# The head of a six-layer cross network: the first column group of x0 through TensorE, the biases loaded later

## The chip, the cores and the metric

The kernel runs on one core of a Trainium2 chip. Its engines are TensorE (matrix multiplications; PE in the profile, PEld for its weight loads), VectorE (DVE), ScalarE (ACT), GpSimd (POOL) and SyncE (SP), which here only issues DMA transfers. ScalarE issues some transfers too. The metric is device microseconds of one execution; lower is better.

## The reference

The input x0 has 4096 rows of 416 values in bf16. Six layers follow, each with a 416x416 weight and a bias:

```python
x = x0
for l in range(ws.shape[0]):
    x = x0 * (x @ ws[l] + bs[l]) + x
return x
```

## The kernel before, in words

The kernel keeps x transposed: features lie on the 128 partitions, rows of x along the free axis. 416 features are three planes of 128 (`NK`) and a remainder of 32 (`R`). The 4096 rows are two halves (`s`) of four column groups (`g`) of 512 (`CW`). `XM[0]` holds the three planes of x0 for all rows, `XR[0]` the remainder, packed so that group g of a half lies on partitions 32g to 32g+31. `XRd` is the same with the upper and lower 64 partitions swapped.

How x0 gets there. Eight transposing loads (`load_x0t`, line 76) on SyncE's queue fill the planes, one for each group of each half; each brings 512 rows by 384 features from DRAM. The remainder of the first half comes by four small loads on ScalarE's queue (`load_xrem0`, line 81) with 64-byte pieces into `xrig`; TensorE transposes these four 128x128 tiles (`x0_rem`, line 157), and VectorE copies them out of PSUM three times (line 160): once to `XR[0]` and twice, by halves, to `XRd`. ScalarE's queue also carries the first layer's weights (line 72) and the biases `bsb` (line 102). The weight's last 32 rows (`WR`, line 88) come on SyncE's queue and are copied on chip to the other three partition groups, two by ScalarE (line 110) and one by GpSimd (line 112).

How TensorE starts. It first runs filler matmuls on a constant tile (line 141), eleven of them: two of 256 columns and nine of 512. Then `bias_setup` transposes the biases by seven small matmuls (lines 149 and 151), and VectorE copies them to `bM` and `bR` (lines 152 and 153). Then comes `first_layer(0)`: for each of three output blocks m three matmuls over the planes k for group 0 (line 214), the remainder's four transposes, the same nine matmuls for group 1, eight row matmuls (line 221, contraction over the 32 remainder features), and then groups 2 and 3, six matmuls to an output block. An output block of two groups is a PSUM tile of two banks; the pool has four such tiles, and a tile is taken again when its last reader is done. ScalarE takes the block out of PSUM with the bias added (line 165), VectorE multiplies by x0 and adds x (lines 166 and 169). The second half and the four middle layers follow in the same manner with 128x32 weight tiles (line 181), and the last layer runs the other way round and writes the output rows (lines 327 to 355).

What sets the order. Each engine runs its instructions in the order of its own queue, which a scheduler has laid out from the program; only instructions with `keep_in_program_order` stay where they are written. Waits are semaphore waits. Transfers share eight semaphore lanes in turn: a transfer waits, on its issuing queue, until the transfer that had its lane eight places earlier has landed. In this program the third transposing load waits in that way for the first one, the fourth for the bias load, and the last of the four remainder loads for the first layer's weights.

The lines that set up the head are these:

```python
load_x0t(0, 0)
load_wm(nc.scalar, 0)
nc.scalar.dma_start(bsb[:], bs[:, :])
load_x0t(0, 1)
load_xrem0()
load_wr0()
nc.scalar.activation(dz[:, 1:2], dz[:, 0:1], ACT.Identity, bias=dz[:, 0:1], scale=1.0)
```

The last of them is there to bring ScalarE's function table into the engine before it is needed.

Of the kernel before, what the change touches and what calls it, by code (L numbers as in the profile page):

```python
# [9 lines left out]
ACT = mybir.ActivationFunctionType  # L10
ALU = mybir.AluOpType
BF16 = mybir.dt.bfloat16
FP32 = mybir.dt.float32
# [3 lines left out]
def kernel(  # L17
# [7 lines left out]
    nc = tc.nc  # L25
    B, D = x0.shape
    L = ws.shape[0]
    P = 128
    NK = 3
    R = D - NK * P  # L30
    assert R == 32 and B == 4096 and D == 416 and L >= 2
    NS = 2
    NG = 4
    CW = 512
# [5 lines left out]
    big = ctx.enter_context(tc.tile_pool(name="big", bufs=1))  # L40
    tpool = ctx.enter_context(tc.tile_pool(name="tpool", bufs=6))
    opool = ctx.enter_context(tc.tile_pool(name="opool", bufs=10))
    psum = ctx.enter_context(tc.tile_pool(name="psum", bufs=4, space=bass.MemoryType.PSUM))

    x0_v = x0.rearrange("(bt p) d -> p bt d", p=P)
    out_v = out.rearrange("(bt p) d -> p bt d", p=P)

    ident = const.tile([P, P], BF16)
    dz = const.tile([P, 2], FP32)
    warm = const.tile([P, CW], BF16)  # L50
# [4 lines left out]
    bsb = const.tile([L, D], BF16)  # L55
# [4 lines left out]
    XLrows = big.tile([P, NBT, D], BF16)  # L60
    scrR = [big.tile([P, 4, P], BF16, name=f"scrR{s}") for s in range(NS)]
    xrem = big.tile([P, 16, R], BF16)
    xrig = big.tile([P, NS, 4, P], BF16)
    XRd = big.tile([P, NS * CW], BF16)
    XM = [big.tile([P, NK, B], BF16, name=f"XM{i}") for i in range(3)]
    XR = [big.tile([P, NS * CW], BF16, name=f"XR{i}") for i in range(3)]

    def col0(s, g):
        return SW * s + CW * g

    def load_wm(eng, l):
        eng.dma_start(WM[:, l], ws[l, 0:NK * P, :].rearrange("(k p) n -> p k n", p=P))

    def load_x0t(s, g):
        c0 = col0(s, g)
        nc.sync.dma_start_transpose(out=XM[0][:, :, c0:c0 + CW], in_=x0[c0:c0 + CW, 0:NK * P])  # L76

    def load_xrem0():
        with nc.allow_non_contiguous_dma(reason="64B row segments"):
            for i in range(4):  # L80
                nc.scalar.dma_start(xrig[:, 0, i, :].rearrange("p (g r) -> p g r", g=NG), x0_v[:, i:16:4, NK * P:D])

    def load_xrem1():
        with nc.allow_non_contiguous_dma(reason="64B row segments"):
            nc.sync.dma_start(xrem[:], x0_v[:, 16:32, NK * P:D])

    def load_wr0():
        nc.sync.dma_start(WR[0:R, 0, :], ws[0, NK * P:D, :])
# [8 lines left out]
    nc.gpsimd.memset(ones[:], 1.0)  # L97
    nc.gpsimd.memset(WD[:], 0.0)

    load_x0t(0, 0)  # L100
    load_wm(nc.scalar, 0)
    nc.scalar.dma_start(bsb[:], bs[:, :])
    load_x0t(0, 1)
    load_xrem0()
    load_wr0()
    nc.scalar.activation(dz[:, 1:2], dz[:, 0:1], ACT.Identity, bias=dz[:, 0:1], scale=1.0)  # L106
    for g in range(1, NG):
        dst, src = WR[32 * g:32 * g + 32, 0, :], WR[0:R, 0, :]
        if g < NG - 1:
# [2 lines left out]
            nc.gpsimd.tensor_copy(dst, src)  # L112
    for g in range(2, NG):
        load_x0t(0, g)
    load_x0t(1, 0)
    load_xrem1()
    for g in range(1, NG):
# [16 lines left out]
    nc.gpsimd.tensor_copy(xrig[:, 1].rearrange("p i (g r) -> p i g r", g=NG), xrem[:].rearrange("p (g i) r -> p i g r", g=NG))  # L134
    fill_wd(1, L)

    wps = psum.tile([P, CW], FP32, tag="ps", name="wps")

    def pe_filler(n, cols):
        for i in range(n):  # L140
            nc.tensor.matmul(wps[:, 0:cols], lhsT=warm[:, 0:P], rhs=warm[:, 0:cols], start=True, stop=True)  # L141

    pe_filler(2, 2 * P)
    pe_filler(8, CW)

    def bias_setup():
        pb = psum.tile([P, 4, 8], BF16, tag="ps", name="pb")
        for m in range(NK):
            nc.tensor.transpose(pb[:, m, 0:L], bsb[0:L, 128 * m:128 * m + 128], ident[0:L, 0:L])
        for g in range(NG):  # L150
            nc.tensor.transpose(pb[32 * g:32 * g + 32, 3, 0:L], bsb[0:L, NK * P:D], ident[0:L, 0:L], tile_position=(0, 32 * g))  # L151
        nc.vector.tensor_copy(bM[:], pb[:, 0:NK, 0:L])  # L152
        nc.vector.tensor_copy(bR[:], pb[:, 3, 0:L])

    def x0_rem(s, tpr):
        for i in range(4):
            nc.tensor.transpose(tpr[:, 128 * i:128 * i + 128], xrig[:, s, i, :], ident[:])  # L157
        for dst, src in ((slice(0, P), slice(0, P)), (slice(64, P), slice(0, 64)), (slice(0, 64), slice(64, P))):
            to = XR[0] if dst == src else XRd
            nc.vector.tensor_copy(to[dst, CW * s:CW * s + CW], tpr[src])  # L160

    def ew_main(l, s, m, h, pt, cur, nxt, pin=False):
        c0 = col0(s, 2 * h)
        t = tpool.tile([P, 2 * CW], BF16, name="t")
        nc.scalar.activation(t[:], pt[:].rearrange("p a b -> p (a b)"), ACT.Identity, bias=bM[:, m, l:l + 1], scale=1.0)  # L165
        prod = nc.vector.tensor_tensor(out=t[:], in0=t[:], in1=XM[0][:, m, c0:c0 + 2 * CW], op=ALU.mult)  # L166
        if pin:
            tc.keep_in_program_order(prod)
        nc.vector.tensor_tensor(out=nxt[:, m, c0:c0 + 2 * CW], in0=t[:], in1=cur[:, m, c0:c0 + 2 * CW], op=ALU.add)  # L169

    def ew_rem(l, s, pr, curR, nxtR):
        tr = tpool.tile([P, 2 * CW], BF16, name="t")
        nc.scalar.activation(tr[:, 0:CW], pr, ACT.Identity, bias=bR[:, l:l + 1], scale=1.0)  # L173
        nc.vector.tensor_tensor(out=tr[:, 0:CW], in0=tr[:, 0:CW], in1=XR[0][:, CW * s:CW * s + CW], op=ALU.mult)  # L174
        nc.vector.tensor_tensor(out=nxtR[:, CW * s:CW * s + CW], in0=tr[:, 0:CW], in1=curR[:, CW * s:CW * s + CW], op=ALU.add)  # L175
# [15 lines left out]
    def mm_rem(l, s, pr, cur, curR):  # L191
        for g in range(NG):
            nc.tensor.matmul(pr[32 * g:32 * g + 32, :], lhsT=WD[:, l, g, :], rhs=curR[:, CW * s:CW * s + CW],  # L193
                             start=True, stop=False, tile_position=(0, 32 * g))
        for k in range(NK):
            for g in range(NG):
                c0 = col0(s, g)
                nc.tensor.matmul(pr[32 * g:32 * g + 32, :], lhsT=WM[:, l, k, NK * P:D], rhs=cur[:, k, c0:c0 + CW],  # L198
                      start=False, stop=(k == NK - 1), tile_position=(0, 32 * g))
# [8 lines left out]
    def first_layer(s):  # L208
        cur, curR, nxt, nxtR = XM[0], XR[0], XM[1], XR[1]

        def full(pt, m, h, gl, after_row):
            c0 = col0(s, 2 * h + gl)
            for k in range(NK):
                nc.tensor.matmul(pt[:, gl, :], lhsT=WM[:, 0, k, 128 * m:128 * m + 128], rhs=cur[:, k, c0:c0 + CW],  # L214
                                 start=(k == 0 and not after_row), stop=(k == NK - 1 and after_row))

        def row(pt, m, h, opens):
            for gl in range(2):
                rg = 32 * ((2 * h + gl) ^ (2 if m == 1 else 0))
                src = XRd if m == 1 else curR  # L220
                nc.tensor.matmul(pt[:, gl, :], lhsT=WR[rg:rg + 32, 0, 128 * m:128 * m + 128],  # L221
                                 rhs=src[rg:rg + 32, CW * s:CW * s + CW],
                                 start=opens, stop=not opens, tile_position=(rg, 0))

        def ph(m):
            return psum.tile([P, 2, CW], FP32, tag="ps", name=f"ph{m}")

        pa = [ph(m) for m in range(NK)]
        if s == 0:
            for m in range(NK):  # L230
                full(pa[m], m, 0, 0, False)
            tp0 = psum.tile([P, CW], BF16, tag="ps", name="tpr")
            x0_rem(0, tp0[:])
            for m in range(NK):
                full(pa[m], m, 0, 1, False)
        else:
            for m in range(NK):
                for gl in range(2):
                    full(pa[m], m, 0, gl, False)
        pb = [ph(0)]  # L240
        row(pa[0], 0, 0, False)
        row(pb[0], 0, 1, True)
        row(pa[2], 2, 0, False)
        row(pa[1], 1, 0, False)
        for m in range(NK):
            ew_main(0, s, m, 0, pa[m], cur, nxt)
        for m in range(NK):
            if m:
                pb.append(ph(m))
            for gl in range(2):  # L250
                full(pb[m], m, 1, gl, m == 0)
        row(pb[1], 1, 1, False)
        row(pb[2], 2, 1, False)
        pr = psum.tile([P, 2, CW], FP32, tag="ps", name="pr")
        mm_rem(0, s, pr[:, 0, :], cur, curR)
        if s == 0:
            x0_rem(1, pr[:, 1, :].bitcast(BF16)[:, 0:CW])
        for m in range(NK):
            ew_main(0, s, m, 1, pb[m], cur, nxt, pin=(s == 0))
        ew_rem(0, s, pr[:, 0, :], curR, nxtR)  # L260

    bias_setup()
    pe_filler(1, CW)
    for s in range(NS):
        first_layer(s)

# [48 lines left out]
    l = LL  # L315
# [97 lines left out]
```

## Time and profile before

| | |
|---|---|
| Median of three runs | 130.97 us (130.72 to 131.04) |
| Profiled execution | 130.71 us |
| Its span, from first to last instruction | 128.9 us |
| Mean granted TensorE clock | 0.998 |
| TensorE busy | 123.1 us, 96% |
| VectorE busy | 107.1 us, 83% |
| ScalarE busy | 86.9 us, 67% |
| GpSimd busy | 5.9 us, 5% |
| 72 matmuls of line 214 (groups of layer 0) | 16.5 us busy |

Times in the profile count from the start of the span. A busy matmul row overlaps the next one, since matmuls are pipelined: the pitch between two, not the duration of one, is what a row of them costs. A line of the timeline has start, length, engine, source line, operation, tile written and tiles read, shape, count, and in brackets how long the engine stood idle before it and what ended that. The chain that ended last is followed back from the last instruction, at each step to what released it.

### The profile page before, as it was taken

To read this page: it belongs to the slowest core of one execution; us is meant where nothing else is said; L and a number is where in the kernel's file an instruction comes from. 1 tells how busy PE (TensorE), PEld (TensorE's weight loads), DVE (VectorE), ACT (ScalarE), POOL (GpSimd) and SP (SyncE) were. 2 spreads that over 40 slices of the span, in tenths; PEclk is the share of its full clock that TensorE was granted. 3 is DMA by queue.
4 is the path that set the end of the run, shared out by engine and by line. 5 is a ranking of instruction groups with operands and counts; after the bars stand their busy time and mean duration, and the time that the engine had idled before them with its cause. 6 is when DMAs were issued, how large, how long until landed. Compare 5 with 4: busy or idle time off the path is not lost.

```text
span 128.9 us, 3973 instructions
## 1 busy us (share of the span) xinstructions
PE 123.1 (96%) x1690; PEld 54.9 (43%) x1690; DVE 107.1 (83%) x197; ACT 86.9 (67%) x99; POOL 5.9 (5%) x18
## 2 busy tenths in 40 slices
PE   6999999999999999999999999999999999999960
PEld 2343443354444444444444444444444445445420
DVE  1032979999999898989898989898989899898991
ACT  0426783987848577848668848668847896569670
POOL 4022200600000000000000000000000000000000
PEclk9999999999999999999999999999999999999999
DMA  3999999999990000000000000000297999995754
GB/s 106 237 203 217 170 158 260 247 328 333 336 299 11 5 0 8 0 0 5 0 5 0 5 0 5 0 5 0 42 166 164 123 219 178 187 323 188 231 179 139
DMA packets 42102, 16.37 MB, mean 127 GB/s; under 512 B 30906, under 2 KB 42084, under 8 KB 42084
## 3 DMA queue, kind: packets, MB, share of 16 engines
q1 hardware_dynamic: 39416, 15.56, 54.6%
q10 hardware_dynamic: 2668, 0.56, 2.3%
q8 instruction: 13, 0.21, 0.7%
q14 instruction: 5, 0.04, 0.1%
HBM read 6.15 MB, written 3.41 MB: 74 GB/s over the span
## 4 chain that ended last, share of the span: by engine, by line
PE 80%; DMA 8%; DVE 5%; issue 2%; SPq 1%; ACT 1%; DVEq 0%
PE pt L181 49%; PE ph L214 9%; DMA XM<-in_x_dram 8%; PE py L327 8%; PE pt L187 5%; PE pr L198 5%; DVE t L355 3%; DVE o L344 2%; PE pr L193 2%; SPq L76 1%; PE py L333 1%; PE ph L221 1%; PE py L336 1%; ACT t L354 1%; PE pr L157 0%
## 5 line engine op out<-in xcount | busy, mean ns | idle before, releaser
L181 PE MATMUL pt<-XM,WM 128*32 128x512 bf16 x1152 | 65.2, 379 | 0.0
L165 ACT ACTIVATE t<-pt,bM 128x1024 bf16<-128x1024 f32 x48 | 49.6, 1115 | 18.3 <-PE pt L187 18.3
L166 DVE TENSOR_TENSOR t<-t,XM 128x1024 bf16<-128x1024 bf16 x60 | 41.4, 690 | 5.3 <-ACT t L165 5.3
L169 DVE TENSOR_TENSOR XM<-t,XM 128x1024 bf16<-128x1024 bf16 x60 | 41.8, 696 | 3.4
L181 PEld LDWEIGHTS <-WM 128*32 128x32 bf16 x1152 | 29.7, 97 | 33.8 <-issue 5.1
L354 ACT CAST t<-py 128x416 bf16<-128x416 f32 (+1 forms) x23 | 14.8, 642 | 4.8 <-PE py L327 2.1
L327 PE MATMUL py<-WM,XM 128*128 128x416 bf16 x96 | 17.7, 340 | 0.0
L214 PE MATMUL ph<-XM,WM 128*128 128x512 bf16 x72 | 16.5, 379 | 0.1
L165 ACT ACTIVATE t<-ph,bM 128x1024 bf16<-128x1024 f32 x12 | 12.5, 1114 | 4.4 <-PE ph L221 4.4
L327 PEld LDWEIGHTS <-XM 128*128 128x128 bf16 x96 | 9.0, 98 | 8.5 <-issue 1.4
L355 DVE TENSOR_TENSOR t<-t,X0rows 128x416 bf16<-128x416 bf16 (+1 forms) x23 | 10.4, 454 | 1.2 <-ACT t L354 1.2
L214 PEld LDWEIGHTS <-WM 128*128 128x128 bf16 x72 | 6.8, 98 | 8.6 <-issue 1.3
L344 DVE TENSOR_TENSOR o<-t,XLrows 128x416 bf16<-128x416 bf16 (+1 forms) x23 | 10.3, 451 | 0.0
L173 ACT ACTIVATE t<-pr,bR 128x512 bf16<-128x512 f32 x10 | 6.4, 684 | 2.7 <-PE pr L198 2.1
L198 PE MATMUL pr<-XM,WM 128*32 128x512 bf16 x120 | 8.2, 379 | 0.0
L187 PE MATMUL pt<-XR,WR 32*128 32x512 bf16 x96 | 7.3, 379 | 0.0
L141 PE MATMUL wps<-warm 128*128 128x512 bf16 (+1 forms) x11 | 4.4, 593 | 1.2 <-DVE warm L94 1.2
L175 DVE TENSOR_TENSOR XR<-t,XR 128x512 bf16<-128x512 bf16 x10 | 4.2, 423 | 0.7
L198 PEld LDWEIGHTS <-WM 128*32 128x32 bf16 x120 | 3.2, 97 | 3.1
L106 ACT ACT_TABLE_LOAD x1 | 1.3, 1283 | 4.3 <-DMA WM<-in_ws_dram 4.3
L174 DVE TENSOR_TENSOR t<-t,XR 128x512 bf16<-128x512 bf16 x10 | 4.2, 418 | 0.0
L152 DVE CAST bM<-pb 128x18 f32<-128x18 bf16 x1 | 0.2, 177 | 4.6 <-PE pb L151 4.6
(39 smaller groups left out, 33.6 us busy)
## 6 DMA issues: line engine op xcount, KB each, us to landing
X0rows<-in_x_dram SPq DMA_DIRECT2D x4, 832.0 KB, 11.6
out_dram<-o SPq DMA_DIRECT2D x9, 208.0 KB, 2.4
WM<-in_ws_dram SPq DMA_DIRECT2D x5, 312.0 KB
out_dram<-o SPq DMA_DIRECT2D x13, 104.0 KB, 1.7
WR<-in_ws_dram SPq DMA_DIRECT2D x4, 130.0 KB, 4.1
WM<-in_ws_dram ACTq DMA_DIRECT2D x1, 312.0 KB
XM<-in_x_dram SPq DMA_TRANSPOSE x8, 4.9
xrig<-in_x_dram ACTq DMA_DIRECT2D x4, 32.0 KB, 4.1
```

The lines of the kernel that those rows point to most:

```text
L165: nc.scalar.activation(t[:], pt[:].rearrange("p a b -> p (a b)"), ACT.Identity, bias=bM[:, m, l:l + 1], scale=1.0)
L166: prod = nc.vector.tensor_tensor(out=t[:], in0=t[:], in1=XM[0][:, m, c0:c0 + 2 * CW], op=ALU.mult)
L169: nc.vector.tensor_tensor(out=nxt[:, m, c0:c0 + 2 * CW], in0=t[:], in1=cur[:, m, c0:c0 + 2 * CW], op=ALU.add)
L173: nc.scalar.activation(tr[:, 0:CW], pr, ACT.Identity, bias=bR[:, l:l + 1], scale=1.0)
L181: nc.tensor.matmul(pts[g // 2][32 * q:32 * q + 32, g % 2, :], lhsT=WM[:, l, k, 128 * m + 32 * q:128 * m + 32 * q + 32], rhs=cur[:, k, c0:c ...
L187: nc.tensor.matmul(pts[g // 2][:, g % 2, :], lhsT=WR[32 * g:32 * g + 32, l, 128 * m:128 * m + 128], rhs=curR[32 * g:32 * g + 32, CW * s:CW ...
L198: nc.tensor.matmul(pr[32 * g:32 * g + 32, :], lhsT=WM[:, l, k, NK * P:D], rhs=cur[:, k, c0:c0 + CW], start=False, stop=(k == NK - 1), tile ...
L214: nc.tensor.matmul(pt[:, gl, :], lhsT=WM[:, 0, k, 128 * m:128 * m + 128], rhs=cur[:, k, c0:c0 + CW], start=(k == 0 and not after_row), sto ...
L327: nc.tensor.matmul(py[:, 0:D], lhsT=cur[:, k, q_cols(q, g)], rhs=WM[:, l, k, :], start=((not closes) and k == 0), stop=(closes and k == NK ...
L344: tc.keep_in_program_order(nc.vector.tensor_tensor(out=o, in0=t, in1=xl, op=ALU.add))
L354: nc.scalar.copy(tv, src)
L355: tc.keep_in_program_order(nc.vector.tensor_tensor(out=tv, in0=tv, in1=X0rows[:, b, :], op=ALU.mult))
```

## The change

Five edits in the head; nothing after the first layer's first half is touched.

First, group 0 of the first half is no longer loaded by a transposing load. Its 512 rows come as one plain load of whole rows into `xg0` (128 partitions, 4 rows of 416 to each). TensorE transposes them by twelve 128x128 transposes, four to each plane, into three bf16 planes of a PSUM tile `tg0`, and VectorE copies each plane to `XM[0]`.

Second, the remainder of those 512 rows is in `xg0` already: GpSimd copies it to `xrig`, and the four small loads bring three quarters of what they brought.

Third, the activation that brings in ScalarE's table stands ahead of the remainder's loads on ScalarE, and behind the weight load.

Fourth, the biases are loaded behind the remainder's loads, after the loads of groups 2 and 3 are written, and `bias_setup` moves from ahead of the first layer to within group 1's matmuls. Its PSUM tile is now a corner of `tg0`, as is that of the first `x0_rem`.

Fifth, group 0's nine matmuls run with the plane k as the outer loop instead of the output block m. One filler of 512 columns, which stood behind `bias_setup`, is gone, and the fillers write to the first output block's PSUM tile, so that no tile is needed for them.

```diff
@@ load_xrem0
-                nc.scalar.dma_start(xrig[:, 0, i, :].rearrange("p (g r) -> p g r", g=NG), x0_v[:, i:16:4, NK * P:D])
+                nc.scalar.dma_start(xrig[:, 0, i, R:P].rearrange("p (g r) -> p g r", g=NG - 1),
+                                    x0_v[:, i + 4:16:4, NK * P:D])
@@ head
-    load_x0t(0, 0)
+    nc.sync.dma_start(xg0[:], x0_v[:, 0:4, :])
     load_wm(nc.scalar, 0)
-    nc.scalar.dma_start(bsb[:], bs[:, :])
     load_x0t(0, 1)
+    nc.scalar.activation(dz[:, 1:2], dz[:, 0:1], ACT.Identity, bias=dz[:, 0:1], scale=1.0)
     load_xrem0()
     load_wr0()
-    nc.scalar.activation(dz[:, 1:2], dz[:, 0:1], ACT.Identity, bias=dz[:, 0:1], scale=1.0)
+    nc.gpsimd.tensor_copy(xrig[:, 0, :, 0:R], xg0[:, :, NK * P:D])
...
     for g in range(2, NG):
         load_x0t(0, g)
+    nc.scalar.dma_start(bsb[:], bs[:, :])
     load_x0t(1, 0)
@@ TensorE's start
-    wps = psum.tile([P, CW], FP32, tag="ps", name="wps")
+    pa0 = [ph(m) for m in range(NK)]
+    tg0 = psum.tile([P, 2, CW], FP32, tag="ps", name="tg0")
+    tgv = [tg0[:, a, :].bitcast(BF16).rearrange("p (b c) -> p b c", b=2) for a in range(2)]
+    planes = [tgv[0][:, 0, :], tgv[1][:, 0, :], tgv[1][:, 1, :]]
...
-        pb = psum.tile([P, 4, 8], BF16, tag="ps", name="pb")
+        pb = tgv[1][:, 0, 0:32].rearrange("p (m l) -> p m l", m=4)
...
+    pe_filler(2, 2 * P)
+    pe_filler(8, CW)
+    for k in range(NK):
+        for i in range(4):
+            nc.tensor.transpose(planes[k][:, 128 * i:128 * i + 128], xg0[:, i, 128 * k:128 * k + 128], ident[:])
+    for k in range(NK):
+        nc.vector.tensor_copy(XM[0][:, k, 0:CW], planes[k])
@@ first_layer
-        pa = [ph(m) for m in range(NK)]
+        pa = pa0 if s == 0 else [ph(m) for m in range(NK)]
         if s == 0:
-            for m in range(NK):
-                full(pa[m], m, 0, 0, False)
-            tp0 = psum.tile([P, CW], BF16, tag="ps", name="tpr")
-            x0_rem(0, tp0[:])
+            for k in range(NK):
+                for m in range(NK):
+                    full(pa[m], m, 0, 0, False, (k,))
             for m in range(NK):
                 full(pa[m], m, 0, 1, False)
+                if m == 0:
+                    x0_rem(0, tgv[0][:, 1, :])
+                elif m == 1:
+                    bias_setup()
...
-    bias_setup()
-    pe_filler(1, CW)
```

In the built program the seven bias transposes stand behind group 1's nine matmuls and the first row matmul, the first of VectorE's three plane copies waits for the last of the twelve transposes, the bias load waits on ScalarE's queue for the lane of group 1's load, the last remainder load for that of the weights, the load of group 3 for that of `xg0`, and the load of group 2 for none.

More of the change, by code (lines that the diff above doesn't have):

```diff
@@ L62 @@
     xrem = big.tile([P, 16, R], BF16)
+    xg0 = big.tile([P, 4, D], BF16, name="xg0")
     xrig = big.tile([P, NS, 4, P], BF16)
@@ L135, with ph @@
     fill_wd(1, L)
-    wps = psum.tile([P, CW], FP32, tag="ps", name="wps")
+    def ph(m):
+        return psum.tile([P, 2, CW], FP32, tag="ps", name=f"ph{m}")
+    pa0 = [ph(m) for m in range(NK)]
+    tg0 = psum.tile([P, 2, CW], FP32, tag="ps", name="tg0")
+    tgv = [tg0[:, a, :].bitcast(BF16).rearrange("p (b c) -> p b c", b=2) for a in range(2)]
+    planes = [tgv[0][:, 0, :], tgv[1][:, 0, :], tgv[1][:, 1, :]]
     def pe_filler(n, cols):
         for i in range(n):
-            nc.tensor.matmul(wps[:, 0:cols], lhsT=warm[:, 0:P], rhs=warm[:, 0:cols], start=True, stop=True)
-    pe_filler(2, 2 * P)
-    pe_filler(8, CW)
+            nc.tensor.matmul(pa0[0][:, 0, 0:cols], lhsT=warm[:, 0:P], rhs=warm[:, 0:cols], start=True, stop=True)
     def bias_setup():
-        pb = psum.tile([P, 4, 8], BF16, tag="ps", name="pb")
+        pb = tgv[1][:, 0, 0:32].rearrange("p (m l) -> p m l", m=4)
         for m in range(NK):
@@ L209, in first_layer, with full @@
         cur, curR, nxt, nxtR = XM[0], XR[0], XM[1], XR[1]
-        def full(pt, m, h, gl, after_row):
+        def full(pt, m, h, gl, after_row, ks=range(NK)):
             c0 = col0(s, 2 * h + gl)
-            for k in range(NK):
+            for k in ks:
                 nc.tensor.matmul(pt[:, gl, :], lhsT=WM[:, 0, k, 128 * m:128 * m + 128], rhs=cur[:, k, c0:c0 + CW],
@@ L223, in row @@
                                  start=opens, stop=not opens, tile_position=(rg, 0))
-        def ph(m):
-            return psum.tile([P, 2, CW], FP32, tag="ps", name=f"ph{m}")
-        pa = [ph(m) for m in range(NK)]
+        pa = pa0 if s == 0 else [ph(m) for m in range(NK)]
         if s == 0:
-            for m in range(NK):
-                full(pa[m], m, 0, 0, False)
-            tp0 = psum.tile([P, CW], BF16, tag="ps", name="tpr")
-            x0_rem(0, tp0[:])
+            for k in range(NK):
+                for m in range(NK):
+                    full(pa[m], m, 0, 0, False, (k,))
             for m in range(NK):
                 full(pa[m], m, 0, 1, False)
+                if m == 0:
+                    x0_rem(0, tgv[0][:, 1, :])
+                elif m == 1:
+                    bias_setup()
         else:
```

## The prediction

> **What bounds the kernel now.** I read the page's engine table first: TensorE is busy 96% of the span and VectorE 83%, so only stretches in which TensorE waits can be won or lost. The chain that ended last says where these are. Its columns are start, length (us) and what ran:
>
> ```profile
> 0.74 4.86 DMA XM<-in_x_dram
> ...
> 5.61 1.44 SPq L76
> ...
> 7.10 5.00 DMA XM<-in_x_dram
> ...
> 12.14 3.40 PE ph L214 x15
> 15.54 0.33 PE ph L221 x4
> 15.87 0.33 PE pr L193 x4
> 16.20 0.65 PE pr L198 x12
> 16.85 0.33 PE pr L157 x4
> 17.18 3.88 PE ph L214 x18
> ```
>
> To 12.14 us the chain is the transposing loads of x0: the first (call the four of the first half t00 to t03) lands at 5.60, only then does SyncE issue t02, and t03 lands at 12.10. From 12.14 to 115.8 the chain is TensorE without a hole. So the change is worth what it does to one moment: when TensorE has done groups 0 and 1 and the row matmuls of line 221 and starts group 2. The timeline shows it:
>
> ```profile
> 1.19 4.45 PE L141 MATMUL wps<-warm 128*128 128x256 bf16 x11 [1.19 <-DVE warm L94]
> ...
> 4.57 0.15 PEld L141 LDWEIGHTS <-warm 128*128 128x128 bf16 x1 [0.28 <-issue]
> ...
> 5.56 0.14 PEld L149 LDWEIGHTS <-bsb 6*128 6x128 bf16 x3 [0.84 <-DMA bsb<-in_bs_dram]
> ...
> 5.84 2.12 PE L214 MATMUL ph<-XM,WM 128*128 128x512 bf16 x9
> ...
> 6.06 0.16 DVE L153 CAST bR<-pb 128x6 f32<-128x6 bf16 x1
> ...
> 8.37 0.10 PEld L157 LDWEIGHTS <-xrig 128*128 128x128 bf16 x1 [0.20 <-DMA xrig<-in_x_dram]
> ...
> 8.62 2.10 PE L214 MATMUL ph<-XM,WM 128*128 128x512 bf16 x9
> 8.64 0.42 DVE L160 COPY XR<-tpr 128x512 bf16<-128x512 bf16 x1 [2.43 <-PE tpr L157]
> ...
> 9.10 0.86 DVE L160 COPY XRd<-tpr 64x512 bf16<-64x512 bf16 x2
> ...
> 11.20 0.55 PEld L214 LDWEIGHTS <-WM 128*128 128x128 bf16 x4 [0.42 <-issue]
> ```
>
> Group 0 runs at 5.84, group 1 at 8.62, group 2 at 11.20, group 3 at 12.14. Three matmuls take 0.65 (15 take 3.40 with their pitch, 0.217 each), so TensorE stood 0.29 before 12.14: group 2 could have begun at 12.14 - 0.65 = 11.49 at no cost. **11.49 is the mark**: each us by which the changed kernel starts group 2 later than that is a us of time, and each us earlier is a gain. Between 5.84 and 11.20 lie 5.36 us, of which 18 x 0.217 + 0.33 (transposes) + 0.54 (rows) + 0.08 is 4.85 work and 0.51 waiting: for the last remainder load at 8.37, and for t01, which is issued at 2.16 and lands 6.4 later, at 8.56.
>
> **The change, part by part.** In the built order I looked for each wait.
>
> Fillers: one of 11 goes. They run at 0.43 a piece (the weight loads at 3.72, 4.15, 4.57 stand that far apart), the last ends at about 5.43, so ten end at 5.0.
>
> xg0, the row load, takes t00's place as SyncE's first issue (0.74). It is 426 KB in 832-byte rows, beside the 320 KB weight load that ScalarE issues at 0.73. Below, the weight load alone: ScalarE's next remainder load, which waits for it, is issued at 3.94, so 3.2 after its issue, 3.95 for xg0. Above, t00's 4.9: 5.64. Both loads share the engines, 746 KB at the 314 to 340 GB/s of the weight load's last half us take about 2.3 from the first byte at 1.8, with some 0.7 to the semaphore (the weight load's packets stop between 3.0 and 3.5): about 5.0. I take 5.2 for the start of the transposes, low 5.0 (fillers), high 5.65.
>
> Twelve transposes of xg0: 0.33 for four (chain, 16.85) makes 0.98 for twelve. Low 0.70 (four weight loads in 0.23 at 16.77), high 1.93, if the clock is still that of the fillers (0.43 against 0.217). I take 0.98, since the weight loads at 5.56 already take 0.09 to 0.10 and not 0.15. The first VectorE copy does not start after plane 0: in the built order its one wait is on the twelfth transpose, the only one that signals, and the other two copies have no wait. So nothing of the transposes is covered. From last transpose to copy 0.25 (8.37 to 8.64), the copy 0.42 (the same form at 8.64), 0.07 to TensorE; the second and third copies run beside group 0's matmuls, three of 0.65 to a plane of 0.42. Group 0 starts at 5.2 + 0.90 + 0.25 + 0.42 + 0.07 = 6.84, a us later than now.
>
> Group 0 ends at 8.8, group 1's first output block at 9.45 (t01 is now issued at 1.35; at 4.9 to 6.4 after that, 6.3 to 7.8, it is in time: its wait is gone).
>
> Table load first, remainder loads after: ScalarE spends 1.28 + 0.29 before the four loads, so they start near 2.8 and not 1.92, and the bias load's 0.70 is gone from ahead of them. The fourth waits for the weight load's semaphore lane, about 4.7 to 5.0. Landing 4.1 to 5.1 after issue: 8.8 to 10.1. I take 9.1, nearest to the last load now (3.94 to 8.35). Needed at 9.45: hidden; at the high end it costs 0.65. They carry a quarter less, so a gain is possible but hidden too. The Pool copy of xg0's remainder (a 128x512 one took 0.79) lies before 6.5: hidden.
>
> So transposes of the remainder 9.45 to 9.78, the other six matmuls to 11.1, where the 0.51 of waiting has vanished. VectorE copies XR and XRd from 9.95 to 11.25.
>
> Biases late: their load now stands behind the fourth remainder load on ScalarE and waits for t01's lane, so it goes out at 6.3 to 7.8, I take 7.4. Landing: low 1.7 (output stores at the end), high 4.4 (this load now, issued at 1.19, used at 5.56, partly behind the weight load in its queue); I take 3.2, that value less the 1.1 behind the weights, so 10.6. ScalarE's WR copies queue behind its issue, to about 9.2, before the rows. The seven bias transposes sit on TensorE after the first row matmul (11.1) and also wait for XRd's last copy, since they write the same PSUM tile: 11.3. They hide the load by 0.7; at its high end (12.2) it costs 0.9. Then 0.28 of transposes (5.56 to 5.84), and the row matmuls of the next PSUM tile wait for the tile that VectorE empties with bM and bR: 0.65 from first transpose to bR's end (5.57 to 6.22), 11.95. Three row matmuls run in that time; four remain, 0.27. Group 2 starts at about **12.27**. Now the bias work ran at 5.56 to 5.84 beside the wait for t00: this cover is gone.
>
> SyncE: t02 and t03 no longer wait for t00 but for nothing and for xg0. With t03's issue one to two us earlier it lands near 11, needed at 12.9: the 0.29 before group 3 is gone, which the mark holds already. The later loads move up too; no TensorE wait after 12.14 asks for one.
>
> Sum: 12.27 - 11.49 = **+0.78**. The profiled run took 130.71 (128.9 span, 1.8 around it): 131.49 on that base. The median of the runs is 130.97, 0.26 above it, and I forecast against that: 131.75. With every low end (5.0, 0.70) it is +0.3, with xg0 at 5.65 and the remainder or bias load at its high end +1.2 to +1.7.
>
> **The rivals.**
> (1) The clock. The fillers run at half rate at least to 4.57 and the weight loads at 5.56 are at full rate; the changed kernel stops its fillers at 5.0 and fills the rest with transposes and a wait of 0.7 for VectorE. If full rate does not come by then, transposes take 0.95 more (+1.73 in all, 132.7); if it has to be earned anew by group 0, as over the fillers' 3.4 us or more, another 1.7 are lost: 134.4. For it: 5.0 is within the stretch in which the change came. Against: nearly all of the work ahead of it stays. The Trainium skill ("TensorE: Matmul & The Clock Gate", Part 4: PE-mode transpose) says that transposes do not count as TensorE activity and that full rate does not engage for them, and gives about 275 ns for one in a kernel. Twelve at that figure would be an estimate of 3.3 us, and the sum +3.1. The trace's four at 16.85 took 0.33 together, amid matmuls, so there full rate held.
>
> (2) Biases late to the end: t01 lands at 7.8, the bias load needs its 4.4, TensorE waits from 11.3 to 12.2 and all else of the block follows: +1.7, 132.7. For: its own row of today. Against: today it stood behind the weights.
>
> (3) Faster: the path starts earlier. If xg0 lands like the weight load alone (3.95) and the fillers reach full rate early and are done, everything to 12.27 moves up by 1.25: 11.02, -0.47, 130.5; t03 (needed at 11.67) is still in time. It decides from a start of the transposes before 4.42. Against: the trace has the fillers at half rate until 4.57.
>
> (4) Nearly nothing: plane copies overlapping the transposes, as the change's words suggest. That would save 8 x 0.082 = 0.65: +0.13, 131.1. The built wait speaks against it.
>
> **How the numbers follow.** Forecast 0.63, its own range 131.2 to 132.2; clock 0.12; late biases 0.13; faster 0.07; nothing 0.05. A measurement of this kernel tells about 0.3%, 0.39 us, from no change. Of the forecast about 0.06 falls under +0.39, with (4) 0.11 the same; some 0.01 of (3) goes there too, and 0.01 of stray to faster: faster 0.07, same 0.12, slower 0.81. The range 131.1 to 133.0 holds the forecast, (2) and the milder half of (1), and leaves out (3) and the full price of (1).
>
> **What would show it.** Right: transposes of xg0 start at 5.0 to 5.5; the first plane copy begins 0.25 after the twelfth; group 0's first matmul at 6.6 to 7.1; no wait for t01 or t03; bias transposes at 11 to 11.5 and a hole of some 0.3 to 0.4 amid the row matmuls; group 2 at 12.0 to 12.6; from there every piece of the chain as long as before. Wrong: matmuls of group 0 at a pitch of 0.43 (rival 1), a bias weight load that waits for its DMA (2), group 0 before 6.0 (3), or a first copy ahead of the last transpose (4).

## The result

The changed kernel is slower by 0.8%: 131.97 us, the median of six runs (131.71 to 132.25), against 131.00 for six runs of the kernel before beside it (130.42 to 131.07). The ratio is 1.0082, with a 95% interval from 1.0062 to 1.0102. The forecast was 131.75, with a range from 131.1 to 133.0. The profiled execution took 132.03 (span 130.2) against 130.71 (span 128.9).

### The profile page after: what moved, and what is told of

The parts are those of the page before. It is cut to its first block, busy times and chain, and to the rows that moved or that the text cites. A ratio compares the mean times of both kernels' runs of the same rounds, so it can differ in the third digit from the quotient of the medians.

```text
span 130.2 us, 3999 instructions
## 1 busy us (share of the span) xinstructions
PE 123.9 (95%) x1701; PEld 55.9 (43%) x1701; DVE 108.3 (83%) x200; ACT 86.8 (67%) x99; POOL 6.6 (5%) x19
## 4 chain that ended last, share of the span: by engine, by line
PE 85%; DVE 6%; DMA 4%; issue 2%; ACT 1%; DVEq 0%
PE pt L195 49%; PE ph L228 12%; PE py L339 8%; PE pt L201 5%; PE pr L212 5%; DMA xg<-in_x_dram 4%; DVE t L367 3%; PE ph L235 2%; DVE o L356 2%; PE pr L207 2%; PE py L345 1%; PE tg L165 1%; PE py L348 1%; ACT t L366 1%; DVE XM L167 0%
## 5 line engine op out<-in xcount | busy, mean ns | idle before, releaser
L167 DVE COPY XM<-tg 128x512 bf16<-128x512 bf16 x3 | 1.1, 418 | 5.2 <-PE tg L165 5.2
L150 PE MATMUL ph<-warm 128*128 128x512 bf16 (+1 forms) x10 | 4.0, 586 | 1.2 <-DVE warm L96 1.2
L112 ACT COPY WR<-WR 32x416 bf16<-32x416 bf16 x2 | 1.1, 536 | 5.7 <-DMA WR<-in_ws_dram 5.7
```

## The profile after

The chain that ended last, of the changed kernel, answers the first fence of the prediction (start, length, what ran):

```profile
0.74 4.66 DMA xg<-in_x_dram
...
5.44 1.10 PE tg L165 x12
...
6.57 0.44 DVE XM L167
...
7.05 2.75 PE ph L228 x12
9.79 0.23 PE tg L171 x4
10.02 1.29 PE ph L228 x6
11.31 0.32 PE ph L235
11.63 0.06 PE tg L155 x3
11.69 0.11 PE tg L157 x4
11.80 1.05 PE ph L235 x7
12.85 3.99 PE ph L228 x18
16.84 0.33 PE ph L235 x4
```

Before, this head was two transposing loads with SyncE between them, and TensorE's chain began at 12.14. Now TensorE, VectorE and the row load stand in one series from 0.74 to the end. There is no transfer in it after 5.40. Group 2 starts at 12.85, where the free mark of before was 11.49: 1.36 later. Behind 12.85 stand 3.99 and 0.33; before, from the mark, it was 15.54 - 11.49 = 4.05 and 0.33. So nothing behind the head gave anything back, and the two profiled times differ by 1.32 us.

The timeline of the changed kernel, from the row load's landing to group 2 (the line numbers are the changed kernel's: 165 the transposes of `xg0`, 167 the plane copies, 228 the groups, 235 the row matmuls, 155 and 157 the bias transposes, 158 and 159 their copies):

```profile
1.26 1.28 ACT L105 ACT_TABLE_LOAD   x1 [1.26 <-PEq L409]
1.47 1.22 ACTq L82 DMA_DIRECT2D xrig<-in_x_dram  x2
2.71 3.30 ACTq L82 DMA_DIRECT2D xrig<-in_x_dram  x2
5.44 1.09 PE L165 MATMUL tg<-ident,xg 128*128 128x128 bf16 x12 [0.24 <-DMA xg<-in_x_dram]
6.57 1.09 DVE L167 COPY XM<-tg 128x512 bf16<-128x512 bf16 x3 [5.16 <-PE tg L165]
7.05 2.75 PE L228 MATMUL ph<-XM,WM 128*128 128x512 bf16 x12 [0.52 <-DVE XM L167]
7.95 0.54 ACTq L117 DMA_DIRECT2D bsb<-in_bs_dram  x1
10.51 0.86 DVE L174 COPY XRd<-tg 64x512 bf16<-64x512 bf16 x2
11.25 0.39 PE L235 MATMUL ph<-XR,WR 32*128 32x512 bf16 x1
11.47 0.22 PE L155 MATMUL tg<-ident,bsb 6*128 6x6 bf16 x3
11.73 0.90 PE L235 MATMUL ph<-XR,WR 32*128 32x512 bf16 x5
11.95 0.15 DVE L159 CAST bR<-tg 128x6 f32<-128x6 bf16 x1
12.22 0.14 PEld L235 LDWEIGHTS <-WR 32*128 32x128 bf16 x4 [0.38 <-issue]
12.46 0.39 PE L235 MATMUL ph<-XRd,WR 32*128 32x512 bf16 x2
12.79 0.39 PE L228 MATMUL ph<-XM,WM 128*128 128x512 bf16 x1
```

Three things are to be seen. VectorE's first plane copy starts at 6.57, behind the twelfth transpose, after 5.16 of waiting: nothing of the transposes is covered. The wait for `t01` and that for the last remainder load are gone from TensorE: group 0, group 1 and the remainder's transposes follow each other from 7.05 to 11.31. And the eight row matmuls, with the bias work among them, run from 11.31 to 12.85; before, they took 0.54.

## The experiments

All kernels were timed in five rounds beside the kernel before, on three chips, where the medians of the kernel before were 130.74 to 130.90 us; the ratio after each time is against the kernel before on the same chip. Edits are to the changed kernel. Next to the times stands when TensorE starts group 2 in the profile, by the chain that ended last, since that is where the loss lies. The timeline has the same start 0.06 to 0.07 earlier; where the chain doesn't hold it (two kernels), as much was added to the timeline's.

**Leaving the biases out.** This kernel leaves the biases of layers 0 to 4 out, to price the bias block as a whole.

```diff
-    nc.scalar.dma_start(bsb[:], bs[:, :])
...
+    nc.gpsimd.memset(bM[:], 0.0)
+    nc.gpsimd.memset(bR[:], 0.0)
...
-                elif m == 1:
-                    bias_setup()
```

> The changed kernel without the bias load, the seven bias transposes and their two copies (bM and bR are set to zero, so the biases of layers 0 to 4 are left out). Theory A, both new blocks stand on TensorE's path: the bias block's hole goes, group 2 starts when the rows behind XRd (11.37 in the changed kernel's profile) are done, near 11.9 instead of 12.85, and the time falls by 0.9 to 1.0 us, to 131.0, about that of before. Rival B, the block costs only its own seven transposes (0.28), and the hole is filled by another wait: 131.7.

Measured: 131.27 (131.19 to 132.06), 1.0046 times before (1.0027 to 1.0066). Its chain that ended last:

```profile
5.49 0.86 PE tg L166 x12
...
6.37 0.43 DVE XM L168
...
6.84 2.75 PE ph L229 x12
...
11.11 0.81 PE ph L236 x8
11.92 3.99 PE ph L229 x18
```

Eight row matmuls take 0.81 here, and 0.32 + 0.06 + 0.11 + 1.05 = 1.54 with the bias block among them: the block costs 0.73, with only 0.17 of transposes in it. Without it group 2 is still 11.92 - 11.49 = 0.43 late.

Not all of this is the row load's path, for the same eight row matmuls took 0.54 before. Here they are before, and then without biases, together with VectorE's last copies ahead of them:

```profile
10.66 0.60 PE L221 MATMUL ph<-XR,WR 32*128 32x512 bf16 x6
10.89 0.38 PE L221 MATMUL ph<-XRd,WR 32*128 32x512 bf16 x2
```

```profile
10.31 0.86 DVE L175 COPY XRd<-tg 64x512 bf16<-64x512 bf16 x2
11.04 0.67 PE L236 MATMUL ph<-XR,WR 32*128 32x512 bf16 x6
11.53 0.39 PE L236 MATMUL ph<-XRd,WR 32*128 32x512 bf16 x2
```

The trace has the start of each one. Before, they start in two sets of four, at 10.66 and 10.89, each set within 0.01 us: two matmuls that read partitions 0 to 63 beside two that read partitions 64 to 127. Without biases they start as two at 11.04, four at 11.31 and two at 11.53. That is three steps instead of two, and 0.27 more. Between the first two and the rest TensorE's queue waits for VectorE's semaphore (11.21), just behind the end of XRd's last copy (11.17): the third and fourth row matmul open the next PSUM tile, which by the prediction's reading of the built program is the one that VectorE has to empty. In the changed kernel the wait at the same place ends with bR's copy (12.10), long after XRd's. So of the 0.43, 0.27 is this third step, and 0.16 is the row load's path, up to the first row matmul (11.11 against 11.49 - 0.54 = 10.95). The copies come late because the remainder's transposes now stand behind the first three of group 1's nine matmuls; no run moves these alone, but where they stand ahead of group 1 (all mends, below) the eight take 0.54 again.

The twelve transposes took 0.86 here and 1.10 in the changed kernel, on the same data and with the same fillers ahead. The weight loads of the two, and of a second profile of the changed kernel (below), tell why. The numbers are least, median and largest duration in ns:

```profile
L166 PEld LDWEIGHTS <-xg x12: 96/98/99, 5.5 to 6.1; 128*128 128x128 bf16 x12
```

```profile
L165 PEld LDWEIGHTS <-xg x12: 97/108/152, 5.4 to 6.3; 128*128 128x128 bf16 x12
```

```profile
L165 PEld LDWEIGHTS <-xg x12: 106/147/147, 5.5 to 6.6; 128*128 128x128 bf16 x12
```

The first is the kernel without biases, the second and third are the changed kernel. The filler's weight loads take 0.15, so the second fence still has some transposes at the fillers' rate and the third has nearly all of them. In the profile of the second fence the change comes amid the transposes: their starts stand 107 ns apart up to 5.95 and 56 ns apart from 6.03. The granted clock that the profile gives from 5 to 8 us is 1.00 in all three, so it does not show this difference.

**The biases early.** The load goes behind the weight load, and `bias_setup` behind the first plane copy, where TensorE waits for VectorE; the bias transposes write a corner of the third output block's PSUM tile.

```diff
     load_wm(nc.scalar, 0)
+    nc.scalar.dma_start(bsb[:], bs[:, :])
...
-    nc.scalar.dma_start(bsb[:], bs[:, :])
     load_x0t(1, 0)
...
-        pb = tgv[1][:, 0, 0:32].rearrange("p (m l) -> p m l", m=4)
+        pb = pa0[2][:, 1, :].bitcast(BF16)[:, 0:32].rearrange("p (m l) -> p m l", m=4)
...
         nc.vector.tensor_copy(XM[0][:, k, 0:CW], planes[k])
+        if k == 0:
+            bias_setup()
...
-                elif m == 1:
-                    bias_setup()
```

> The changed kernel with the bias load back behind the weight load and the bias transposes between the plane transposes and group 0, where TensorE waits for VectorE's first copy (PSUM: the idle bank of the third output block). Theory A: the seven transposes fit into the wait of 0.5 if the bias load lands by 6.5, bM and bR delay the second plane copy by 0.35 of which 0.15 reaches group 0, and the late block's 0.9 to 1.0 is gone: time 131.1 to 131.2, the same as before. Rival B (block hardly costs anything): 131.8. Rival E, the bias load lands late behind the row load (beyond 7.0) and TensorE waits for it: 131.6 or more, with that wait in the profile.

Measured: 131.29 (131.20 to 131.49), 1.0044 (1.0028 to 1.0060): within 0.02 us of the kernel without any biases, but still slower than the kernel before, where the expectation had the same time. From its chain:

```profile
11.26 0.81 PE ph L237 x8
12.07 3.99 PE ph L230 x18
```

The bias transposes run at 6.23 to 6.56, within the wait for VectorE's first copy, and group 0 starts at 6.81. Then the row matmuls take 0.81, as without biases. So it is the place of the block that costs, not its work. The 0.15 by which 12.07 is later than 11.92 is a wait for a remainder load (0.18, less 0.03 by which group 0 starts earlier):

```profile
9.73 0.10 PEld L173 LDWEIGHTS <-xrig 128*128 128x128 bf16 x1 [0.18 <-DMA xrig<-in_x_dram]
```

**The changed kernel once more**, unaltered, to see whether the rate of the transposes belongs to the kernel or to the execution.

> The changed kernel once more, for its time on the same chip as the others and a second profile. In the profiles so far the twelve plane transposes ran at full rate in two kernels (weight loads of 98 ns) and at half rate in two others (151 ns), with the same fillers ahead of them. Theory F: the moment at which the full rate comes is set by the execution and not by the kernel, so this profile may show another rate than the first of the same kernel (median 108 ns, a mixture), and its group 2 starts between 12.6 (all at full rate) and 13.2 (all at half rate), with the time 119.2 above that start. Rival G, the rate is set by the kernel: again a mixture, group 2 at 12.85.

Measured: 132.37 (131.73 to 132.42), 1.0101 (1.0078 to 1.0124). The six times form two groups: 131.73 and 131.84, and four from 132.36 to 132.42. The profiled one, 132.39, is of the second, and it is the one with weight loads of 147 ns. Its chain:

```profile
5.53 1.40 PE tg L165 x12
...
7.43 2.75 PE ph L228 x12
...
13.24 0.32 PE ph L228
```

The transposes take 1.40 for the 0.86 without biases, 0.54 more, and the groups of times lie 0.6 apart. Group 0 runs at its full pitch, 2.75 for its twelve, in all three profiles. So when TensorE comes to its full rate is a matter of the execution, and the changed kernel pays up to 0.54 for it. (The six times of the first measurement, 131.71 to 132.25, do not fall into two groups.)

**A PSUM tile of its own for plane 0**, so that the first copy need not wait for the eight transposes of the other planes.

```diff
-    planes = [tgv[0][:, 0, :], tgv[1][:, 0, :], tgv[1][:, 1, :]]
+    planes = [pa0[1][:, 1, :].bitcast(BF16)[:, 0:CW], tgv[1][:, 0, :], tgv[1][:, 1, :]]
```

> The changed kernel with the first plane in a PSUM tile of its own (the idle bank of the second output block), so that its copy waits for four transposes and not for twelve. Theory A: the first copy starts near 5.9, group 0's matmuls follow the transposes at 6.45 instead of 7.05, and the 0.6 us come off the time in full if the remainder has landed by the time its transposes are asked for, near 9.0: 131.4. Rival C, the remainder's fourth load is just in time in the changed kernel (its lane waits for the weights, issue at 5.63, landing 4.1 later, 9.7): then the transposes wait for it and only 0 to 0.2 us are gained: 131.8 to 132.0, with a wait for the remainder's DMA in the profile.

Measured: 131.79 (131.59 to 131.95), 1.0077 (1.0059 to 1.0095). The timeline has the copy where it was expected, and released by the first four transposes, which now write another tile:

```profile
5.98 0.42 DVE L167 COPY XM<-ph 128x512 bf16<-128x512 bf16 x1 [4.56 <-PE ph L165]
```

But this profile has weight loads of 151 ns (median) for the transposes, the remaining eight kept TensorE until 6.79, and group 2 starts at 12.71, only 0.14 earlier than in the changed kernel's first profile. TensorE waits for no remainder load, so rival C's cause did not come, though the time is near its range. Slow is to be compared with slow: from the first transpose to group 2 it is 7.38 here (5.33 to 12.71) and 7.71 in the second profile (5.53 to 13.24). At the slow rate the tile is worth 0.33. What it is worth at full rate stays open, since no profile here shows it at that rate by itself.

**Output blocks outside, planes inside**, in group 0, as it was before.

```diff
-            for k in range(NK):
-                for m in range(NK):
-                    full(pa[m], m, 0, 0, False, (k,))
+            for m in range(NK):
+                full(pa[m], m, 0, 0, False)
```

> The changed kernel with group 0's nine matmuls in the old order, output block outside and plane inside. Theory A: the first block then waits for the second copy (0.44 behind the first) and the third (0.88), its second matmul at 7.5 and its third at 7.95, and group 0 ends 0.45 us later: 132.4. Rival D, a later wait (the remainder's landing, XRd's copies) takes the 0.45: no change, 132.0.

Measured: 132.42 (132.00 to 132.67), 1.0117 (1.0094 to 1.0140). The medians put this 0.45 above the changed kernel, but 0.05 above its second measurement. The chain shows what the order is worth:

```profile
7.47 2.98 PE ph L228 x12
```

Group 2 starts at 13.51. Group 0 starts where it does in the second profile of the changed kernel (7.43, also with slow transposes) and takes 2.98 instead of 2.75. Its second and third matmul start 0.33 apart instead of 0.22, each behind its plane's copy (the copies stand 0.33 to 0.34 apart, and not the 0.44 of the expectation). So the plane-outer order is worth 0.23; that the rest of the 0.45 is the rate of the transposes is likely, since they are slow in this profile too, but not shown by itself.

**The table load back behind the remainder's loads.**

```diff
-    nc.scalar.activation(dz[:, 1:2], dz[:, 0:1], ACT.Identity, bias=dz[:, 0:1], scale=1.0)
     load_xrem0()
     load_wr0()
+    nc.scalar.activation(dz[:, 1:2], dz[:, 0:1], ACT.Identity, bias=dz[:, 0:1], scale=1.0)
```

> The changed kernel with ScalarE's table load back behind the remainder's loads. The four remainder loads then get other semaphore lanes, none of which waits for the weights. Theory A: the remainder lands well ahead of its use near 9.4 in either case, so nothing changes: 131.8 to 132.1 (within 0.15 of the changed kernel on the same chip). Rival C, the remainder's fourth load is just in time: up to 0.3 faster where group 0 is early.

Measured: 131.83 (131.71 to 132.54), 1.0091 (1.0066 to 1.0115): no difference from the changed kernel that these runs can tell. In its profile the four loads are issued from 1.24 to 3.63 and group 2 starts at 12.52 with fast transposes. That the profiled time is 132.54 has another cause: with the other order the load of group 2, on SyncE's queue, waits for the weights and goes out at 5.55 and not at 4.16, the later transposing loads come later, and TensorE waits for one of the second half until 19.46:

```profile
11.62 7.84 DMA XM<-in_x_dram
```

**The weights behind the row load, by themselves**: both on SyncE's queue, so that the row load goes out ahead of them.

```diff
-    load_wm(nc.scalar, 0)
+    load_wm(nc.sync, 0)
```

> The changed kernel with one edit: the first layer's weights on SyncE's queue behind the row load, not on ScalarE's beside it. Theory A: the row load lands 3.2 after its issue, near 4.0, not 4.7, and the plane transposes begin when the fillers end, 5.0 instead of 5.45: group 2 moves up by 0.4 to 0.45, and the time to 131.5 to 131.9 at the mixture of rates that the changed kernel shows (131.7 to 132.4). Rival H, the weights (landing near 5.6) or group 1's load, each a place later on the queue, take it back: no change.

Measured: 131.73 (131.54 to 131.88; four runs), 1.0074 (1.0049 to 1.0099). The row load lands 4.0 after its issue instead of 4.66, with two remainder loads issued beside it (0.73 to 1.82), and the transposes start right behind the fillers, with weight loads of 98 ns. Group 0 starts at 6.24, 0.60 earlier than in the kernel without biases, whose transposes ran at the full rate too. Its first weight load now waits for the weights:

```profile
5.95 0.10 PEld L228 LDWEIGHTS <-WM 128*128 128x128 bf16 x1 [0.40 <-DMA WM<-in_ws_dram]
6.24 2.89 PE L228 MATMUL ph<-XM,WM 128*128 128x512 bf16 x12 [0.52 <-DVE XM L167]
```

That wait costs nothing, since the first matmul is released later, by VectorE's copy. What rival H named in the second place did cost a little: group 1's load, a place later on the queue, lands 6.5 after its issue at 1.79, and group 1's first matmul starts at 8.32, 0.36 behind the one before and not 0.22. So the twelve take 2.89 instead of 2.75. Group 2 starts at 12.19, and the profiled time is 131.54, within the expectation.

**All mends together.** The biases early and plane 0's own tile as above, the remainder by three loads instead of four, its transposes ahead of group 1, and the weights behind the row load.

```diff
-            for i in range(4):
-                nc.scalar.dma_start(xrig[:, 0, i, R:P].rearrange("p (g r) -> p g r", g=NG - 1),
-                                    x0_v[:, i + 4:16:4, NK * P:D])
+            for g in range(1, NG):
+                nc.scalar.dma_start(xrig[:, 0, :, R * g:R * g + R], x0_v[:, 4 * g:4 * g + 4, NK * P:D])
...
-    load_wm(nc.scalar, 0)
+    load_wm(nc.sync, 0)
...
-                full(pa[m], m, 0, 1, False)
                 if m == 0:
                     x0_rem(0, tgv[0][:, 1, :])
+                full(pa[m], m, 0, 1, False)
```

> All mends together: biases early, the first plane in a PSUM tile of its own, three remainder loads by group instead of four, their transposes ahead of group 1, and the first layer's weights on SyncE's queue behind the row load instead of beside it on ScalarE's. Theory A: the row load lands near 4.5 and not at 5.4, the plane transposes start when the fillers end (5.0), group 0 near 6.3, group 1 follows the remainder's transposes near 8.6, rows at 10.55, group 2 at 11.1 (11.4 with transposes at half rate): 130.3 to 130.6, faster than before by 0.3 to 0.6 if group 1's load, now third on the queue, lands by 8.6. Rival H, the row load lands no earlier alone, or the later place of group 1's load takes it back: group 2 at 11.6 or more, 130.8 or more, no faster than before.

Measured: 130.78 (130.39 to 132.33; twelve runs), 1.0016 (0.9987 to 1.0045): as fast as the kernel before and no faster. The row load lands 3.2 after its issue and the weights 4.3 after theirs, by the list of transfers (kilobytes of 1024 bytes, so 416 and 312 for the prediction's 426 and 320, and us from issue to landing):

```profile
xg<-in_x_dram SPq DMA_DIRECT2D x1, 416.0 KB, 3.2
...
WM<-in_ws_dram SPq DMA_DIRECT2D x1, 312.0 KB, 4.3
```

Group 0's matmuls begin only at 6.67, although the transposes follow the fillers at once: they ran at the fillers' rate (147 ns), and the bias transposes behind them take until 6.67. The remainder's transposes stand ahead of group 1 here, XRd's last copy ends at 10.32, and the row matmuls take what they took before:

```profile
10.91 0.54 PE ph L236 x8
```

Group 2 starts at 11.45, the mark of before.

**The same with two fillers less**, since the transposes now wait for the fillers.

```diff
-    pe_filler(8, CW)
+    pe_filler(6, CW)
```

> The kernel with all mends and two fillers of 512 columns fewer, so that they end at 4.15 instead of 5.0; the row load has landed at 3.94 there. Theory A: the plane transposes start at 4.15, group 0 near 5.8 (the weights land at 5.55), group 2 at 10.6 to 10.9 unless the loads of groups 1 to 3 are now the later ones: 129.9 to 130.4, faster than before by 0.5 to 1.0. Rival F: with fewer fillers ahead the full rate comes later too, group 0 runs at half rate (0.43 a matmul, up to 1.9 more) and the time is 130.8 or more. Rival I: the transposing loads of groups 2 and 3 take over as in the kernel before, group 2 or 3 waits for its DMA: 130.4 to 130.8.

Measured: 130.62 (129.85 to 131.39; twelve runs), 0.9987 (0.9966 to 1.0008): not shown to be faster. The row load lands 3.4 after its issue and the transposes start at 4.18. Group 0 runs at its full pitch from its second matmul (6.17), so rival F did not come. TensorE begins group 2's first matmul at 10.70, by the chain's count at about 10.77, as expected: 0.72 ahead of the mark. Then it gives part of this back, as the chain shows:

```profile
10.71 6.47 DMA XM<-in_x_dram
```

The timeline has the wait:

```profile
17.23 2.97 PE L229 MATMUL ph<-XM,WM 128*128 128x512 bf16 x12 [0.19 <-DMA XM<-in_x_dram]
```

A load of the second half is issued at 10.71, behind all that stands on SyncE's queue, and lands at 17.19; TensorE is there before it. This is rival I's kind of wait, one half later than it was looked for. The profiled time, 130.31, is 0.40 under that of before though the head is 0.72 shorter, and the median is 0.12 under (130.74 before).

**One relation over all of these.** Where TensorE waits for no transfer after group 2's start, the profiled time is that start plus 119.2 to 119.4:

| Kernel | Group 2 starts (us) | Profiled time (us) | Difference |
|---|---|---|---|
| before (free mark) | 11.49 | 130.71 | 119.22 |
| all mends | 11.45 | 130.68 | 119.23 |
| no biases | 11.92 | 131.27 | 119.35 |
| biases early | 12.07 | 131.22 | 119.15 |
| weights behind | 12.19 | 131.54 | 119.35 |
| plane 0's own tile | 12.71 | 131.86 | 119.15 |
| changed | 12.85 | 132.03 | 119.18 |
| changed, second profile | 13.24 | 132.39 | 119.15 |
| blocks outside | 13.51 | 132.67 | 119.16 |
| table load late (waits until 19.46) | 12.52 | 132.54 | 120.02 |
| two fillers less (waits until 17.19) | 10.77 | 130.31 | 119.54 |

## Why the prediction was right, and where its sizes were off

The mechanism is the one forecast: a mark at 11.49 that group 2 misses, first by the series of row load, transposes and copy, then by the bias block amid the row matmuls, and an unchanged chain behind. Step by step, forecast against the changed kernel's profile:

- The transposes start at 5.44 and not 5.2. The row load landed 4.66 after its issue, at 5.40, near the top of the bounds; with the weights behind it on its own queue it took 3.2 to 4.0. The estimate from bytes and bandwidth left too little for the two loads beside each other, and its terms (1.8, 2.3 and 0.7) add up to 4.8, not to the 5.0 that it has. This is 0.24 of the miss.
- Twelve transposes up to the first copy: 1.13 for 1.15. The size was right by chance: it is 0.88 at the full rate (no biases) and 1.42 at the fillers' (second profile). Rival 1 in its mild form was put as something that happens or not, with 0.12. It happens in part of the executions, and fully in four of the six of the second measurement, if the two groups of times mean that; it costs up to 0.54 and not the rival's 0.95.
- The first copy waits for the twelfth transpose, and one plane's copy covers the others: right. Rival 4, overlap, did not come; the tile of its own shows that it needs another PSUM tile.
- Group 0 at 7.05 for 6.84; the only reason is the row load. Then the matmuls to the row matmuls ran without a wait, as forecast: 11.31 for 11.1.
- "Table load first": the step said that the remainder's loads start near 2.8. They did not wait for it. Two were issued from 1.47 to 2.69, the first of them while the table load still ran (1.26 to 2.54). The conclusion, hidden, held; the table load back in its old place made no difference.
- Biases: issued at 7.95 (7.4), no wait for their load, transposes at 11.47 behind XRd's last copy (11.3), bR done at 12.10 (11.95). Rival 2 did not come.
- "Four remain, 0.27": TensorE starts again at 12.22 and reaches group 2 at 12.79 to 12.85, 0.43 later against bR's end than forecast. This is the largest miss, and the term of the sum that was mis-sized. The four do not run as one set: two start at 12.25 and the XRd pair at 12.46, for all four read partitions 64 to 127, and those that they ran beside before (partitions 0 to 63) are done. They take 0.57 (12.22 to 12.79) in place of 0.27; the rest is the start behind bR's copy, 0.12 after its end. The prediction had seen the wait for the PSUM tile, but not that it leaves the last matmuls without others to run beside. Nor had it seen that the tile's earlier readers, XRd's copies, do the same without any bias block: 0.81 for the eight where its sum has 0.54.

So 12.85 instead of 12.27 is 0.21 up to group 0, 0.43 in the rows, and 0.06 the other way between. At full rate, by the kernel without biases, the loss is 0.16 on the row load's path up to the row matmuls (forecast 0.15), 0.27 for their third step (not in the forecast) and 0.73 for the bias block (forecast 0.63), 1.16 together; the forecast was 0.78. The medians differ by 0.97 in the first measurement and by 1.47 in the second. On the profile's own base the forecast was 131.49 against 132.03, 0.54 short; that the median is only 0.22 above the forecast comes from the medians' smaller step, and is luck.

Rival 3, faster, decides from a start of the transposes before 4.42, as the prediction put it. The last experiment had them at 4.18 with the biases mended too, and the head was then indeed shorter than before, by 0.72. What the rival overlooked is the second half's load, which takes back 0.32 of it in the profile; the median of that kernel is not told apart from before.

The Trainium skill ("TensorE: Matmul & The Clock Gate", Part 1, What's actually happening) says that TensorE comes to full speed at the end of a free-running window of about 3.4 us, so that the moment shifts between executions of one kernel. The two profiles of the unaltered kernel, 108 and 147 ns for the median weight load, agree that it shifts; no run here shows the window itself. The Trainium skill ("TensorE: Matmul & The Clock Gate", Part 4: PE-mode transpose) says that full rate does not engage for transposes and gives about 275 ns for one. The runs here differ on the rate: the starts of the twelve stand 56 ns apart without biases and 107 ns apart in the second profile, and in the first the change comes amid them. The record of one transpose is 0.22 to 0.31 us long here, but they overlap, so that twelve took 0.86 to 1.40 and not the 3.3 that the prediction estimated from that figure.

What stays open: what plane 0's own tile is worth at full rate, and what it would bring to move the remainder's transposes ahead of group 1 by themselves. No version tried here is shown to be faster than the kernel before.

## What to carry to other kernels

Work that sits in a wait is free only there: the bias block's 0.17 us of transposes cost 0.73 once they stood between matmuls that needed their PSUM tile back, and nothing that could be measured when put into another wait of TensorE. Matmuls that run beside each other lose that when one of them has to wait for its tile, so look who empties it last. Price a moved block by the chain it opens (what it waits for, who copies it out, what must be started again) and not by its busy time. Replacing a transposing load by TensorE transposes puts landing, transposes and a copy in series, and its gain has to come from an earlier landing; then look which later transfer the faster head will run into.

## What the runs showed of the hardware

- The same kernel, with the same fillers, reached TensorE's full rate within its transposes in one profile and only behind them in another (median weight load 108 and 147 ns); that is worth up to 0.54 us of 132. The granted clock in the profile is 1.00 there in both.
- ScalarE's queue sent out a transfer at 1.47, within its own table load of 1.26 to 2.54.
- A row load of 416 KB took 4.66 us from issue to landing beside a weight load of 312 KB on another queue, and 3.2, 3.4 and 4.0 in three kernels with the weight load behind it on its own queue; in the last, two remainder loads were issued beside it.
- Eight row matmuls over 32 features took 0.54 us when they started in two sets of four (two on partitions 0 to 63 beside two on 64 to 127), and 0.81 when they started as two, four and two.
- A transposing load of the second half landed 6.5 (two fillers less) and 7.8 us (table load late) after its issue, when others were under way.
